# Sixteen squares of the feed-forward stage moved to POOL, one store for the last block, and a new written order

## The chip, the cores and the metric

The kernel runs on one core of a Trainium2 chip. It uses five engines that run side by side and meet through semaphores: PE (matmuls), DVE (the vector engine), ACT (the scalar engine), POOL (GpSimd) and SP, which here only issues DMAs. The metric is the device time of one execution in microseconds. The kernel before took 110.79 us (median of three runs, 110.61 to 112.53).

## What is computed

Two stages, the first feeding the second. The attention stage maps each query and key vector to a feature vector of 64 products and works with those linearly; the second stage is a feed-forward layer whose activation is the square of the positive part.

```python
def phi(x):                                   # 32 numbers -> 8 x 8 products
    a = np.einsum('rd,bhsd->bhsr', S1, x)
    b = np.einsum('rd,bhsd->bhsr', S2, x)
    return np.einsum('bhsi,bhsj->bhsij', a, b).reshape(*x.shape[:-1], r * r)
q_p, k_p = (phi(q), phi(k))                   # 4 batches, 4 heads, 1088 tokens, 64 features
kv = np.einsum('bhsf,bhsd->bhfd', k_p, v)
z = np.sum(k_p, axis=2)
num = np.einsum('bhsf,bhfd->bhsd', q_p, kv)
den = np.einsum('bhsf,bhf->bhs', q_p, z)[..., None] + 1e-06
x = num / den                                 # then laid out as 4352 tokens x 128
h = x @ w_in                                  # 128 -> 2048
r = np.maximum(h, 0.0)
g = r * r
out = g @ w_out                               # 2048 -> 128, float32
```

## The kernel before

**Attention.** The four batches are worked one after the other, overlapping. For batch b, `ldk`, `ldq` and `ldv` load keys, queries and values through SP's queue; `tk` and `tq` (L532 to L546, L697) transpose on DVE; `ksk` projects keys on PE; `kr` (L572) transposes the projections out of PSUM on DVE; `kp` (L580, L621) forms the 64 products on DVE, for one part of batch 0 on POOL; `vp` (L516, L519) copies the values beside a column of ones on POOL; `kv` (L643) accumulates on PE. Batches 0 and 1 form the query features from matmuls (`qr`, `qa` on ACT, `qp` at L752 on DVE). Batches 2 and 3 ("fold") go through memory: `ab` holds both projections, `zm`, `zt`, `zk`, `zb`, `dt`, `dr`, `dx` (POOL, L880) and `da` (L886) work the denominator in, `wr` stores to scratch memory, `rdA` (SP) and `rdB` (POOL) read it back repeated, and `qp2`, `qp3` (L927) multiply on DVE. `num` multiplies with `kv` on PE, `mx` and `tx` divide and transpose for batches 0 and 1, and `xe` puts the result as bf16 into `xT`, the input of the second stage. Small constants are made at the start: `zc` (L341 to L346) is eight scalings and two memsets on POOL.

**Feed-forward.** The 4352 tokens are cut into ten blocks, 256 tokens, seven times 512 and twice 256 (`SIZES`). Block n has up to nine steps m. A step is four operations, named in the order as `m1.n.m`, `r.n.m`, `g.n.m` and `m2.n.m`: `m1` (L1056) multiplies with two (for short blocks four) columns of tiles of `w_in` into a 128x1024 PSUM tile `h`; `r` (L1066 on ACT, L1068 on DVE) takes the positive part to bf16; `g` squares it (L1074 on ACT, L1076 on DVE); `m2` (L1090) multiplies with `w_out` and accumulates in PSUM, in the order of m. There are four buffers each for `r` and `g`, three for `h` and one accumulator for all blocks but the last. After the last step, `oe` (L1116) transposes the block out of PSUM to one of three output buffers `osb` on DVE, and `st` (L1126) stores it, four stores for each batch that the block touches. Block 9 is the exception: its `m2` (L1085) writes tokens in rows, and it is copied and stored in two halves (L1103, L1108).

**Order.** The order is written out. `PLAN` (L40 to L90) is one list of items `name:engine:buffers`; `Graph.run` (L124) emits each operation on the engine and into the buffers given there. Every engine, and every DMA queue, works through its own items in the order of the list, and waits where an input or a buffer is not there yet. The pairs of numbers at each `add(...)` are costs that only the program that found the order uses; they emit nothing. `HEAT` (L19) is a list of matmuls on zeros, by columns, that fill PE's time before the feed-forward stage.

Of the kernel before, what the change touches and what calls it, by code (L numbers as in the profile page):

```python
# [18 lines left out]
HEAT = [512] * 9 + [256] * 15  # L19
# [33 lines left out]
m1.1.3:PE:h1 g.1.0:ACT:g0 kp1.4:DVE qp1.1.0:DVE oe0:DVE:osb0 g.1.1:DVE:g1 ldq2.0:SP qp1.1.1:DVE vp1.1:POOL kv1.1:PE kve1.0:DVE r.1.3:ACT:r2 tk2.1:DVE
m1.1.5:PE:h2 r.1.5:ACT:r3 m2.1.0:PE:o0 ldv2.1:SP ldv2.0:SP tk2.0:DVE kve1.1:ACT m1.1.2:PE:h0 m1.1.4:PE:h1 kve1.2:ACT m2.1.1:PE g.1.3:DVE:g2
r.1.2:ACT:r1 m1.1.7:PE:h2 r.1.7:ACT:r0 r.1.4:ACT:r2 g.1.2:ACT:g3 tq2.0:DVE num1.0:PE:a0 st0.0.0:SP mx1.0:DVE:den0 ksk2:PE:h0 qr2:PE:h2 ab2:ACT
tx1.0:PE:a0 ldv2.2:SP m1.1.6:PE:h1 r.1.6:ACT:r1 xe1.0:ACT kr2:DVE m2.1.2:PE qr1.2:PE:h0:h2 qa1.2.0:ACT:A2 qa1.2.1:ACT:A1 ldv2.4:SP g.1.5:DVE:g0
ldv2.3:SP vp2.0:POOL ldk3.0:SP g.1.4:DVE:g1 vp2.1:POOL m2.1.3:PE kp2.0:DVE wr2.1.3:SP m1.2.4:PE:h1 r.2.4:ACT:r3 wr2.1.2:SP kp2.4:DVE m2.1.4:PE
tk3.1:DVE qp1.2.0:DVE kv2.0:PE:a0 qp1.2.1:DVE kv2.1:PE g.2.4:ACT:g3 kve2:ACT m1.2.0:PE:h1 r.2.0:ACT:r2 wr2.1.0:SP wr2.1.1:SP m1.2.2:PE:h0 m2.1.5:PE
tk3.0:DVE m1.2.1:PE:h2 zm2:DVE g.1.7:DVE:g2 ldq3.0:SP r.2.2:ACT:r3 g.1.6:DVE:g1 zt2:PE:a0 zk2:DVE tq3.0:DVE m1.2.6:PE:h1 m2.1.6:PE ldv3.4:SP zb2:PE:a0
r.2.6:ACT:r0 ldv3.2:SP dt2:DVE m2.1.7:PE oe1:DVE:osb1 ldv3.1:SP g.2.0:ACT:g0 m1.2.3:PE:h0 r.2.1:ACT:r1 num1.1:PE:h1.1 dr2:DVE ldv3.0:SP mx1.1:DVE:den1  # L60
num1.2:PE:a0 st0.0.3:SP r.2.3:ACT:r2 g.2.1:ACT:g1 qr3:PE:h2 ab3:ACT rdB2.544:POOL ksk3:PE:h0 st0.0.2:SP rdB2.0:POOL ldv3.3:SP g.2.2:ACT:g2
st1.256.3:SP dx2:POOL da2:DVE wr2.0.2:SP wr2.0.3:SP kr3:DVE m2.2.0:PE:o0 g.2.3:ACT:g0 mx1.2:DVE:den2 tx1.1:PE:h1.1 xe1.1:ACT m2.2.1:PE st1.256.1:SP
m1.2.7:PE:h2 r.2.7:ACT:r1 kp3.0:DVE m2.2.2:PE kp3.4:DVE m1.2.5:PE:h0 r.2.5:ACT:r3 g.2.5:DVE:g1 m2.2.3:PE m1.3.2:PE:h1 r.3.2:ACT:r2 g.2.6:DVE:g2
wr2.0.0:SP vp3.0:POOL kv3.0:PE:a0 m2.2.4:PE m1.3.1:PE:h2 g.2.7:DVE:g0 vp3.1:POOL r.3.1:ACT:r3 g.3.1:DVE:g3 m1.3.0:PE:h0 r.3.0:ACT:r0 m2.2.5:PE
wr2.0.1:SP tx1.2:PE:h1.1 m2.2.6:PE g.3.2:DVE:g1 m1.3.3:PE:h2 st0.0.1:SP m2.2.7:PE oe2:DVE:osb2 g.3.0:DVE:g2 m1.3.6:PE:h0 r.3.3:ACT:r1 kv3.1:PE zm3:DVE
g.3.3:DVE:g0 m1.3.5:PE:h2 zt3:PE:h1.0 r.3.6:ACT:r3 m1.3.4:PE:h0 m2.3.0:PE:o0 st1.256.0:SP kve3:ACT rdA2.0:SP zk3:DVE qp2.0:DVE st1.256.2:SP zb3:PE:a0
wr3.1.3:SP r.3.5:ACT:r2 m2.3.1:PE dt3:DVE dr3:DVE dx3:POOL r.3.4:ACT:r0 wr3.1.1:SP g.3.4:ACT:g2 num2.0:PE:h2 st2.768.2:SP m2.3.2:PE m1.3.7:PE:h0
xe2.0:ACT wr3.1.0:SP wr3.1.2:SP m2.3.3:PE r.3.7:ACT:r1 xe1.2:DVE m1.4.0:PE:h1 r.4.0:ACT:r0 m2.3.4:PE g.3.5:DVE:g3 m1.4.1:PE:h2 m2.3.5:PE da3:DVE
st2.1088.2:SP g.3.6:DVE:g1 m1.4.2:PE:h0 m2.3.6:PE rdA2.544:SP r.4.1:ACT:r2 r.4.2:ACT:r3 g.3.7:DVE:g0 qp2.1:DVE m1.4.5:PE:h1 st2.768.1:SP m2.3.7:PE
r.4.5:ACT:r1 g.4.0:DVE:g2 m1.4.4:PE:h2 num2.1:PE:h0 m1.4.3:PE:h1 r.4.4:ACT:r0 oe3:DVE:osb0 st2.1088.0:SP xe2.1:ACT wr3.0.3:SP m2.4.0:PE:o0  # L70
m1.4.6:PE:h2 g.4.1:DVE:g3 m2.4.1:PE g.4.2:DVE:g1 g.4.5:DVE:g0 r.4.3:ACT:r2 g.4.4:DVE:g2 wr3.0.2:SP m1.5.0:PE:h0 wr3.0.0:SP g.4.3:DVE:g3 m2.4.2:PE
r.4.6:ACT:r3 g.4.6:DVE:g1 m1.5.5:PE:h1 m2.4.3:PE m1.4.7:PE:h2 r.5.0:ACT:r1 m2.4.4:PE r.4.7:ACT:r0 wr3.0.1:SP m1.5.1:PE:h0 r.5.5:DVE:r2 m2.4.5:PE
m1.5.2:PE:h1 g.5.0:DVE:g3 rdB3.0:POOL g.4.7:DVE:g2 r.5.1:ACT:r3 r.5.2:ACT:r1 rdA3.0:SP m2.4.6:PE m1.5.3:PE:h2 qp3.0:DVE m2.4.7:PE oe4:DVE:osb1
rdB3.544:POOL rdA3.544:SP m1.5.4:PE:h0 g.5.2:DVE:g0 r.5.3:ACT:r0 st4.2176.3:SP g.5.1:ACT:g1 num3.0:PE:h1 xe3.0:DVE r.5.4:ACT:r1 m2.5.0:PE:o0
g.5.3:DVE:g2 m1.5.6:PE:h2 g.5.5:DVE:g3 st4.1792.0:SP st4.1792.1:SP st2.768.0:SP m2.5.1:PE m1.6.0:PE:h1 st2.1088.1:SP st2.1088.3:SP r.5.6:ACT:r3
m2.5.2:PE g.5.4:DVE:g1 m1.5.7:PE:h0 g.5.6:DVE:g0 r.6.0:ACT:r0 qp3.1:DVE m2.5.3:PE m1.6.1:PE:h2 st3.1280.0:SP m2.5.4:PE g.6.0:DVE:g2 r.5.7:ACT:r2
# [74 lines left out]
def pe(t):  # L151
    return (t, t + 0.17)
# [3 lines left out]
def kernel(  # L156
# [1021 lines left out]
```

## Time and profile before

| | |
|---|---|
| runs | 110.79 us median (110.61 to 112.53) |
| profiled execution, own time | 110.52 us |
| its span, first to last instruction | 108.7 us |
| granted TensorE clock, mean | 0.997 |
| POOL copies `vp` of 128x512 | 7, median 614 ns |
| DVE squares `g` | 56, mean 688 ns |
| ACT squares `g` of 128x1024 | 11, mean 1066 ns |
| ACT `r` of 128x1024 | 63, mean 1032 ns (13 in a row take 12.29 us) |

The span runs from the first to the last instruction on the chip; the execution's own time also holds what lies around it, 1.8 us here. Busy times add up the durations of instructions; an instruction starts some 0.08 us before the one ahead of it on its engine has ended, so durations of single instructions are a little longer than their spacing. An instruction that has started and then waits for something inside its engine counts as busy.

### The profile page before, as it was taken

The page shows a single profiled execution, that of the slowest core. Times are in us where ns is not written, and L with a number is a line of the kernel's source. Part 1 is how long each engine was busy: PE and PEld are TensorE (multiplying, and loading weights), DVE is VectorE, ACT ScalarE, POOL GpSimd, SP SyncE. Part 2 cuts the span into 40 slices and gives each one's busy share as a digit, 9 for nine tenths or more (in the row PEclk, how much of TensorE's full clock was granted, in tenths as well). Part 3 has the DMA queues.
Part 4 walks back from the last instruction along what each step waited for, and adds up shares of the span by engine and source line. Part 5 has one row for each costly group of instructions (what it writes and reads, how often), then busy time and mean ns, then how long its engine had stood idle before and what let it go on. Part 6 is the DMA issues. An engine that isn't in the chain of part 4 may idle for free.

```text
span 108.7 us, 3616 instructions
## 1 busy us (share of the span) xinstructions
PE 98.1 (90%) x1438; PEld 56.9 (52%) x1438; DVE 94.1 (87%) x175; ACT 87.6 (81%) x123; POOL 31.4 (29%) x72
## 2 busy tenths in 40 slices
PE   5968999999999997899899999998999999997920
PEld 2355786766655373565546334443444445575920
DVE  5388499999999999699999989997999999996730
ACT  2226463979999999879889998989899999999900
POOL 4914993560005378015800099000000000000000
PEclk9999999999999999999999999999999999999998
DMA  2896999994164189993472358878244000336641
GB/s 53 225 214 195 359 178 252 283 247 140 18 148 178 52 240 205 205 215 80 68 222 64 103 141 229 233 206 201 48 77 80 1 0 0 54 55 104 114 76 39
DMA packets 27025, 15.23 MB, mean 140 GB/s; under 512 B 19712, under 2 KB 24448, under 8 KB 27008
## 3 DMA queue, kind: packets, MB, share of 16 engines
q1 hardware_dynamic: 23976, 11.58, 43.1%
q0 software_dynamic: 2272, 3.28, 15.0%
q8 instruction: 11, 0.18, 0.8%
q10 hardware_dynamic: 760, 0.14, 0.6%
q14 instruction: 6, 0.05, 0.1%
HBM read 13.25 MB, written 2.79 MB: 147 GB/s over the span
## 4 chain that ended last, share of the span: by engine, by line
DVE 43%; PE 27%; issue 8%; SPq 8%; DMA 6%; POOL 1%; ACT 1%; DVEq 1%; POOLq 0%
DVE g L1076 15%; PE o L1090 9%; PE h L1056 6%; DVE kp L580 6%; SPq L1126 4%; DMA vin<-in_v_dram 4%; DVE osb L1116 3%; DVE kT L532 3%; DVE qp L927 2%; PE h L643 2%; DVE qp L752 2%; DVE kt L572 2%; PE h L716 2%; DVE qT L697 2%; DVE xs L1013 2%
## 5 line engine op out<-in xcount | busy, mean ns | idle before, releaser
L1066 ACT ACTIVATE r<-h 128x1024 bf16<-128x1024 f32 x63 | 60.9, 1032 | 4.1 <-PE h L1056 2.2
L1090 PE MATMUL o<-g,w_out 128*128 128x512 bf16 (+1 forms) x144 | 38.3, 356 | 2.2 <-issue 1.1
L1056 PE MATMUL h<-xT,w_in 128*128 128x512 bf16 (+1 forms) x156 | 39.0, 350 | 0.4 <-ACT xT L1031 0.2
L1076 DVE TENSOR_TENSOR g<-r 128x1024 bf16<-128x1024 bf16 x56 | 36.2, 688 | 0.5 <-ACT r L1066 0.2
L1056 PEld LDWEIGHTS <-w_in 128*128 128x128 bf16 x160 | 17.3, 115 | 14.4 <-issue 2.1
L1090 PEld LDWEIGHTS <-w_out 128*128 128x128 bf16 x144 | 13.2, 97 | 14.9 <-issue 5.7
L1074 ACT ACTIVATE g<-r 128x1024 bf16<-128x1024 bf16 (+1 forms) x13 | 12.8, 998 | 0.2
L516 POOL COPY vp<-vin 128x512 f32<-128x512 f32 x7 | 5.2, 769 | 19.2 <-PE h L564 10.4
L914 POOL DMA_DIRECT2D Bq<-scr x16 | 9.0, 595 | 2.2 <-DMA scr<-ab 2.2
L580 DVE TENSOR_TENSOR kp<-kt 128x1024 f32<-128x1024 f32 (+1 forms) x6 | 8.5, 1435 | 0.0
L752 DVE TENSOR_TENSOR qp<-h,A 128x256 f32<-128x256 f32 (+3 forms) x16 | 6.3, 428 | 2.1 <-ACT A L738 2.0
L738 ACT COPY A<-h 128x256 f32<-128x256 f32 (+3 forms) x16 | 5.4, 406 | 2.8 <-PE h L716 2.1
L353 PE MATMUL o<-zero 128*128 128x256 bf16 (+1 forms) x24 | 6.1, 398 | 1.2 <-DVE mk L276 1.2
L1116 DVE STREAM_TRANSPOSE osb<-o 128x512 f32<-128x512 f32 (+1 forms) x9 | 5.8, 648 | 1.2 <-DMA out_dram<-osb 0.8
L716 PE MATMUL h<-qT,SR 32*64 32x192 f32 (+2 forms) x176 | 6.4, 340 | 0.0
L643 PEld LDWEIGHTS a<-vp,kp 128*32 128x32 f32 x432 | 4.5, 109 | 2.6 <-issue 2.5
L927 DVE TENSOR_TENSOR qp<-qp,Bq 128x1088 f32<-128x1088 f32 x4 | 5.2, 1288 | 0.6 <-DMA qp<-scr 0.6
L643 PE MATMUL a<-vp,kp 128*32 128x33 f32 x432 | 5.2, 198 | 0.5 <-POOL vp L519 0.3
L697 DVE STREAM_TRANSPOSE qT<-qin 128x1088 f32<-128x1088 f32 (+5 forms) x7 | 5.5, 803 | 0.0
L880 POOL COPY dnT<-dnr 128x288 f32<-128x288 f32 x2 | 1.3, 674 | 13.0 <-DVE dnr L875 8.7
L519 POOL COPY vp<-vtl 32x128 f32<-32x128 f32 x6 | 5.0, 836 | 0.2
L1068 DVE TENSOR_SCALAR r<-h 128x1024 bf16<-128x1024 f32 x4 | 4.8, 1215 | 0.0
(114 smaller groups left out, 105.5 us busy)
## 6 DMA issues: line engine op xcount, KB each, us to landing
Bq<-scr POOLq DMA_DIRECT2D x16, 136.0 KB, 5.1
qp<-scr SPq DMA_DIRECT2D x8, 272.0 KB, 4.7
vin<-in_v_dram SPq DMA_DIRECT2D x16, 128.0 KB, 4.5
kin<-in_k_dram SPq DMA_DIRECT2D x3, 544.0 KB, 4.0
qin<-in_q_dram SPq DMA_DIRECT2D x3, 544.0 KB, 5.0
out_dram<-osb SPq DMA_DIRECT2D x17, 64.0 KB, 1.9
scr<-ab SPq DMA_DIRECT2D x16, 34.0 KB, 2.2
kin<-in_k_dram SPq DMA_DIRECT2D x2, 256.0 KB, 3.2
```

The costliest lines, as they stand in the source:

```text
L580: (nc.vector if e == "DVE" else nc.gpsimd).tensor_tensor(out=kp[i][:, k0:k1].rearrange("p j h (x y) -> p (j h) x y", y=R), in0=v[:, :, 1, ...
L643: nc.tensor.matmul(t[p : p + KW, 33 * (h // 2) : 33 * (h // 2) + 33], kp[i][:, j, h, KW * f : KW * f + KW], vp[i][:, h, j, :], start=(j == ...
L697: nc.vector.transpose(qT[i][:, 32 * c0 : 32 * c1], qin[i][:, 32 * c0 : 32 * c1])
L716: nc.tensor.matmul(at(hb[h // 2])[lo : lo + 64, 512 * s + 256 * x : 512 * s + 256 * x + ns[s]], SR[32 * h : 32 * h + 32, x].rearrange("p x ...
L752: nc.vector.tensor_tensor(out=o, in0=pv, in1=av, op=ALU.mult)
L914: (nc.sync if e == "SP" else nc.gpsimd).dma_start(out=Bq[i][64 * m : 64 * m + 64, pr, s0:s1], in_=scr[i][1][8 * (2 * pr + m) : 8 * (2 * pr ...
L1056: nc.tensor.matmul(at(hb)[:, c : c + N], w_in[:, 512 * (ct // E) : 512 * (ct // E) + 512].rearrange("p (c e) -> p e c", e=E)[:, ct % E], x ...
L1066: nc.scalar.activation(o, s, ACTF.Relu)
L1074: nc.scalar.activation(at(gb)[:, 0 : W * N], r, ACTF.Square)
L1076: nc.vector.tensor_tensor(out=at(gb)[:, 0 : W * N], in0=r, in1=r, op=ALU.mult)
L1090: nc.tensor.matmul(at(ob)[:, 0:N], w_out[:, ct, :], at(gb)[:, N * w : N * w + N], start=(ct == 0), stop=(ct == CT - 1))
L1116: nc.vector.transpose(at(sbuf)[:, 0:N], at(ob)[:, 0:N])
```

## The change

- Sixteen of the 69 squares go to POOL: `g.1.0`, `1.3`, `1.4`, `1.6`, `2.4`, `2.6`, `3.2`, `3.5`, `3.6`, `4.5`, `5.0`, `5.1`, `6.0`, `6.3`, `6.6` and `7.5`. DVE keeps 42 of its 56, ACT 11 of its 13. On POOL they are the same multiplication of `r` with itself.
- Block 9 is copied out of PSUM at once (`oe9`) and stored with one DMA (`st9.0`). For this the columns of `xT` for the last 256 tokens stand in another order, so that a row of the store is 1024 bytes instead of 512.
- All stores are issued by SP; three were on ACT.
- There are five output buffers `osb` instead of three.
- The matmuls on zeros are 18 of up to 512 columns (8640 columns in all) instead of 24 (8448 columns).
- The whole order is new. Among other things `zc` moves from the start to behind `g.1.0` on POOL, `vp0.0` goes to ACT and `vp0.1` to POOL, `kp0.7` and `SKw` come ahead of the loads of the weights, `num0.0` comes ahead of `qr0.2`, six `r` instead of five are on DVE (3.1, 3.5, 5.1, 6.0, 6.6 and 8.0), and `tq1.0` comes ahead of `qp0.1`.
- A new mode `foldp` and its tables are added, but no batch uses it; some of the planner's costs are changed.

```diff
-HEAT = [512] * 9 + [256] * 15
+HEAT = [512] * 9 + [448] * 1 + [512] * 4 + [192] * 1 + [512] * 2 + [320] * 1
...
-        "r": one("r", NR), "g": one("g", NR), "osb": one("osb", 3), "den": one("den", 3), "A": one("A", 3),
+        "r": one("r", NR), "g": one("g", NR), "osb": one("osb", 5), "den": one("den", 3), "A": one("A", 3),
...
-                    fn(xT[:, t1 + 288 : t1 + 544].rearrange("p (x t c) -> p x c t", x=2, c=4),
-                       at(nb)[:, 528:784].rearrange("p (x c t) -> p x c t", x=2, c=4))
+                    fn(xT[:, t1 + 288 : t1 + 544].rearrange("p (x t c) -> p c x t", x=2, c=4),
+                       at(nb)[:, 528:784].rearrange("p (c x t) -> p c x t", x=2, c=4))
...
-                    nc.vector.tensor_tensor(out=at(gb)[:, 0 : W * N], in0=r, in1=r, op=ALU.mult)
+                    (nc.vector if e == "DVE" else nc.gpsimd).tensor_tensor(out=at(gb)[:, 0 : W * N], in0=r, in1=r, op=ALU.mult)
...
-            for x in range(N // 128):
-                c0 = (n0 - S * b) // 32 + 4 * x
...
-                    fn(at(sbuf)[:, 0:128], at(ob)[:, 128 * x : 128 * x + 128])
...
-                        out=out[S * b : S * b + S, :].rearrange("(t c) d -> t c d", c=C)[:, c0 : c0 + 4, :],
-                        in_=at(sbuf)[:, 0:128])
+            c0, w = (n0 - S * b) // 32, N // 32
+            sbuf = Buf("osb")
...
+                fn(at(sbuf)[:, 0:N], at(ob)[:, 0:N])
...
+                    out=out[S * b : S * b + S, :].rearrange("(t c) d -> t c d", c=C)[:, c0 : c0 + w, :].rearrange(
+                        "t (c x) d -> t c (x d)", x=2),
+                    in_=at(sbuf)[:, 0:N])
+            add(f"st{n}.0", {"SP": (0.65, 3.0)}, f_st, [o_oe], uses=[sbuf], dma=0.4)
...
-                if n >= len(SIZES) - 2:
-                    al["ACT"] = (0.55, 3.0)
```

The new order of POOL from block 1 on, and of DVE from `oe0` to `oe7`, read out of the new list:

```
POOL  z1 vp1.0 vp1.1 g.1.0 zc g.1.4 g.1.3 g.1.6 vp2.0 vp2.1 g.2.4 vp3.0 rdB2.0 dx2 rdB2.544 g.2.6
      vp3.1 g.3.2 g.3.5 g.3.6 dx3 rdB3.0 g.4.5 g.5.0 g.5.1 rdB3.544 g.6.0 g.6.3 g.6.6 g.7.5
DVE   oe0 qp1.1.1 qp1.1.0 tk2.0 tk2.1 g.1.2 mx1.0 tq2.0 g.1.5 kr2 tk3.1 kp2.0 tk3.0 kp2.4 g.2.2
      qp1.2.1 zm2 qp1.2.0 zk2 tq3.0 dt2 dr2 oe1 da2 mx1.1 kr3 kp3.0 mx1.2 r.3.1 g.3.1 kp3.4 r.3.5
      oe2 zm3 kve3 zk3 qp2.0 dt3 dr3 g.3.4 da3 g.3.7 qp2.1 g.4.0 oe3 g.4.1 xe2.1 g.4.2 g.4.3 g.4.6
      g.4.4 r.5.1 g.4.7 qp3.0 oe4 xe3.0 g.5.3 g.5.5 g.5.4 r.6.0 g.5.6 g.5.7 qp3.1 oe5 g.6.1 g.6.2
      r.6.6 g.6.4 g.6.5 g.7.1 g.6.7 g.7.0 oe6 g.7.2 g.7.3 g.7.4 r.8.0 g.7.6 g.8.0 g.7.7 g.8.2 oe7
```

173 lines of the change are left out of this document (102 added, 71 removed).

## The prediction

> **What bounds the kernel now.** I read the busy shares first, then the slices, the chain, and windows over the two stretches that the change works in.
>
> ```profile
> PE 98.1 (90%) x1438; PEld 56.9 (52%) x1438; DVE 94.1 (87%) x175; ACT 87.6 (81%) x123; POOL 31.4 (29%) x72
> ...
> DVE 43%; PE 27%; issue 8%; SPq 8%; DMA 6%; POOL 1%; ACT 1%; DVEq 1%; POOLq 0%
> ```
>
> DVE carries 43% of the chain and is 87% busy; POOL is 29% busy and, by the slices, empty after 69 us. Moving squares there looks free. The windows cut at the block copies: `oe0` ends near 28.5, `oe3` at 68.2, `oe7` at 100.1.
>
> ```profile
> 28.50:68.20 39.70, 37.88 (x719) 20.41 (x716) 37.69 (x71) 37.13 (x52) 16.59 (x26) 1.00 0.63 150
> 68.20:100.10 31.90, 30.70 (x179) 15.69 (x178) 30.18 (x46) 30.83 (x36) 0.00 (x0) 1.00 0.40 86
> ```
>
> The columns are length, then PE, PEld, DVE, ACT and POOL busy. In both stretches PE, DVE and ACT are all within 3 us of full, so a microsecond added to any of the three lengthens the stretch by nearly that much.
>
> **Is POOL independent of DVE?** Three moments in the timelines say no (start, duration, instruction):
>
> ```profile
> 34.54 1.03 DVE L1076 TENSOR_TENSOR g<-r 128x1024 bf16<-128x1024 bf16 x1
> 34.42 0.61 POOL L516 COPY vp<-vin 128x512 f32<-128x512 f32 x1
> ...
> 62.66 0.68 DVE L1076 TENSOR_TENSOR g<-r 128x1024 bf16<-128x1024 bf16 x1
> 62.69 0.92 POOL L880 COPY dnT<-dnr 128x288 f32<-128x288 f32 x1 [8.67 <-DVE dnr L875]
> ...
> 47.51 0.42 POOL L880 COPY dnT<-dnr 128x288 f32<-128x288 f32 x1 [4.37 <-DVE den L1010]
> 47.69 0.56 DVE L1013 TENSOR_TENSOR xs<-h,rec 128x384 bf16<-128x384 f32 x1
> ```
>
> The POOL copy ends at 34.42 + 0.61 = 35.03; the square begun at 34.54 ends at 35.57, 0.54 us later, which is what a square (0.65 alone) needs after its start-up: it stood still until POOL was done. At 62.69 it is the other way: POOL's copy takes 0.92 instead of 0.42 because the square holds it. At 47.69 nothing is held: that DVE operation takes one input from PSUM. So a DVE instruction with **both inputs in SBUF** and a POOL instruction that reads SBUF exclude each other for their whole length. In that class on DVE are the squares `g` (0.60 us from start to start in a run), `kp1` to `kp3` (1.07 to 1.33), `qp2`, `qp3` (1.21) and the product of `da`. Outside it are `oe` (0.64), `r` (1.14), `xe` (0.63), transposes and whatever reads PSUM. POOL's DMA issues hold nobody: squares beside them at 64.5 to 67.6 take the usual 0.68.
>
> The Trainium skill, "SBUF — State Buffer", section "Who interferes with whom", states this as an exclusive lock between a VectorE instruction with two SBUF inputs and any GpSimd instruction that reads SBUF; the rows agree for copies, and no row here has a POOL TENSOR_TENSOR beside such a DVE instruction. By it the forecast's mechanism holds; if it held for copies only, the first rival would be the result.
>
> **Price of one square on POOL.** The trace has none. The nearest row is a POOL product of two SBUF inputs, running beside DVE work of the free class:
>
> ```profile
> 10.41 1.07 POOL L621 TENSOR_TENSOR kp<-kb,ka 128x512 f32<-128x512 f32 x1
> ```
>
> Twice the elements give 2.14 us, the upper end. If bf16 halves it, as on DVE (0.60 for 1024 bf16 against 1.21 for 1088 f32), it is 1.07, the lower end. I take 2.1: same operation, same two reads.
>
> The Trainium skill, "GPSIMD Engine Reference", section 3.1, gives 4497 ns for 2048 f32 elements, so an estimate of 2.25 us here, and its section 4.1 advises against such work on this engine; by that figure the sum would be about 1.5 us longer.
>
> **The sum, against the profiled execution's 110.52 us** (0.27 under the median 110.79 of the runs shown).
>
> *From `oe3` to `oe7`, 31.9 us now.* DVE's own work in the new order: 25 squares x 0.60, 4 `r` x 1.14, `qp3.0` and `qp3.1` 2.4, 4 `oe` x 0.64, 2 `xe` x 0.63 = 25.8 us (now 30.2). ACT: 28 `r` x 0.95 (13 in 12.29 us), one square 1.06, `xe3.1` 1.3 = 29.0; PE 32 pairs of second and first matmuls x 0.87 and two `num` x 0.6 = 29.0. Without the lock the stretch would take some 29.5. With it, I walk down the two orders by hand, t counted from the end of `oe3`; DVE and POOL take turns where both wait:
> - square 4.5 holds the lock 0.6 to 2.7; `g.4.2`, due at 1.2 after `xe2.1`, stands 1.5
> - 5.0 holds 5.1 to 7.2; `r.5.1` runs, `g.4.7` stands 1.0
> - 5.1 holds 7.8 to 9.9; `qp3.0` stands 2.1
> - 6.0 holds 15.9 to 18.0; `g.5.7` stands 2.1
> - 6.3 holds 19.8 to 21.9; `oe5` runs, `g.6.1` stands 1.5
> - 6.6 holds 24.9 to 27.0; `g.6.5` stands 2.1
> - 7.5 holds 30.6 to 32.7; `g.7.3` stands 2.1
>
> Together 12.4 us, so 25.8 + 12.4 = 38.2: **+6.3**. Even with the best alignment the locked classes alone need 15 + 2.4 + 7 x 2.1 = 32.1 us: no gain is possible here at that price.
>
> *From `oe0` to `oe3`, 39.7 us now.* DVE loses nine squares (5.4), `kve1.0` and `xe1.2` (0.5), gains `r.3.1`, `r.3.5` (2.3) and `kve3` (about 0.5): relief 3.2. Stalls: 1.0 none (beside `qp1.1`, `tk2`); 1.4 holds `g.1.5` 1.9; 1.3 holds `kp2.0` 0.7; 1.6 holds `kp2.4` 1.5; `vp2.0`, now right behind, 0.3 more than today; `zc`, eight operations of 0.30 to 0.37 moved here from the start, 0.2; 2.4 none (beside `dt2`, `dr2`); 2.6 holds `g.3.1` 1.0; 3.2, 3.5 and 3.6 in a row hold `qp2.0` 2.1 and `g.3.4` 0.9. Together 8.6, less 3.2 = +5.4; half of DVE's 2.0 us of pauses there absorbs 1.0: **+4.4**.
>
> *Start.* `vp0.0` changes places with `vp0.1`; `kp0.7` comes ahead of the weights; `num0.0` no longer stands behind `qr0.2` (1.07 us of PE); `tq1.0` (0.54) can fill DVE's pause at 11.4 to 13.0. Between -1.1 and +0.7 (a late gate for the weights); I take **-0.5**. Zero matmuls: 24 become 18, 8448 columns become 8640, in PE time that waits for loads anyway: 0. `zc`'s old place (2.2 to 4.8) was idle. Should a weight come late instead, the row "waits for w_in" shows 0.3 today.
>
> *`osb` 3 to 5.* It removes this wait, which sits inside the 31.9 and which the walk does not have:
>
> ```profile
> 99.41 0.72 DVE L1116 STREAM_TRANSPOSE osb<-o 128x512 f32<-128x512 f32 x1 [0.83 <-DMA out_dram<-osb]
> ```
>
> Next late after it is the square itself, so it brings nothing of its own beyond the walk.
>
> *End.* Two copies (0.28 each) become one of twice the width, between 0.28 and 0.45. But the four stores of block 8 (two of them on ACT now) all stand ahead of `st9.0` on SP: `oe8` ends 103.69, four issues of about 0.45 end near 105.5, `st9.0` takes 0.64 to 106.15. Today ACT's `st9.1` is issued until 106.16. **0**, between -0.9 (SP free at once) and +1 (older stores still queued on SP). The changed x columns of the last 256 tokens keep the size of their copy (0.76): 0. The new planner costs and the `foldp` branch emit nothing here.
>
> 110.5 - 0.5 + 4.4 + 6.3 = 120.7, say **121 us**.
>
> **Rivals.**
> 1. *No lock for a POOL TENSOR_TENSOR, or squares that always fall beside free work.* Then the relief is kept: 2.4 in the late stretch (31.9 to 29.5, ACT and PE the next bounds), 2.5 of the 3.2 in the early one (ACT sheds only two `r` there), 0.5 at the start: 105.1. For it: the order places 1.0 and 2.4 beside long runs of free DVE work. Against: the held copies, and that seven squares x 2.1 find only 8.4 us of free DVE work in the late stretch. It decides from a mean stall under 0.3 us per square. Chance 0.16.
> 2. *Squares near the lower end, 1.07 us.* The stalls of the walk shrink to 0.4 + 0 + 4 x 1.0 + 0.4 = 4.8: the late stretch takes 30.6, the early one about as long as now, 109 to 111 in all. For it: DVE's bf16 rate. Against: no POOL row shows a type that goes faster. Chance 0.16.
> 3. *The order degenerates*: a late square on POOL makes PE, whose second matmuls run in block order, wait beside DVE, and stalls average a full 2.1: 16 x 2.1 = 33.6 less 7.6 of relief: up to 136. Waits overlap, so I give all beyond 127 a chance of 0.07, inside the slower case.
>
> **How the numbers follow.** Forecast and third rival 0.68 together, rivals 1 and 2 0.16 each. Two per cent is about what a measurement of this kernel can tell (its runs lie between 110.61 and 112.53). Faster 0.16, within 2% 0.16, slower 0.68. The range from 107.5 to 127 leaves out most of rival 1 and the far tail; it takes in both ends of the square's price. The forecast's own range is 115 to 127.
>
> **What would show it.** Right: POOL squares of 2.1 us or more in the groups, DVE squares (now 688 ns on average) near 1 us, with some near 2.7; DVE's busy time above 100 us although it does less, since a held instruction counts as busy; the stretch from `oe3` to `oe7` near 38 us. Wrong: DVE squares still near 0.7 us and DVE under 90 us (rival 1), or POOL squares near 1.1 (rival 2). The prediction fails if long free runs on DVE line up with the POOL squares more often than my walk has it.

## The result and the profile after

The changed kernel takes **120.96 us** (median of 4 runs, 118.84 to 122.96); the kernel before, in the same job, 111.66 (110.61 to 113.07). The ratio is 1.079, 95% interval 1.054 to 1.104: slower, by about 9 us. The forecast was 121. The profiled execution is the longest of the four, 122.96 us, with a span of 121.2 us against 108.7 before. Executions over 1.5% longer than the fastest of the same kernel, here two of the four, stand outside the ratios.

The page of the changed kernel, in the lines that answer to those of before (busy shares, the clock row of the slices, the chain, and the two groups of squares; L1112 is the line of `g` that was L1076):

```profile
PE 99.6 (82%) x1419; PEld 56.4 (47%) x1432; DVE 103.2 (85%) x163; ACT 85.3 (70%) x117; POOL 66.3 (55%) x90
...
PEclk9999999999999999999999999998599999999999
...
DVE 30%; issue 16%; PE 15%; POOL 11%; ACT 11%; SPq 6%; DMA 6%; ACTq 1%; DVEq 0%; POOLq 0%
...
L1112 POOL TENSOR_TENSOR g<-r 128x1024 bf16<-128x1024 bf16 x16 | 33.1, 2076 | 22.7 <-PE o L1126 9.7
...
L1112 DVE TENSOR_TENSOR g<-r 128x1024 bf16<-128x1024 bf16 (+1 forms) x42 | 37.3, 916 | 2.3 <-ACT r L1102 1.2
```

The DVE squares of the kernel before:

```profile
L1076 DVE TENSOR_TENSOR g<-r 128x1024 bf16<-128x1024 bf16 x56 | 36.2, 688 | 0.5 <-ACT r L1066 0.2
```

DVE has 14 squares fewer and is busy for 9.1 us **more** (94.1 before): 42 squares now take 916 ns on average, 56 took 688. That is the mark of instructions that have started and are held. POOL's 16 squares take 2.08 us each. PEclk shows one dip to half speed, which is followed up below.

Windows cut as before, at the ends of `oe0`, `oe3` and `oe7`; I call the four pieces front, early, late and tail (columns: length, then busy time of PE, PEld, DVE, ACT, POOL with counts, clock, DMA share, GB/s):

```profile
0.00:32.64 32.64, 25.43 (x562) 17.06 (x566) 24.28 (x55) 16.52 (x31) 15.43 (x41) 1.00 0.71 175
32.64:72.49 39.85, 36.67 (x640) 19.86 (x640) 38.12 (x65) 35.43 (x49) 34.14 (x39) 1.00 0.52 136
72.49:112.34 39.85, 32.93 (x176) 16.00 (x178) 36.53 (x38) 29.39 (x34) 16.78 (x11) 0.96 0.41 87
```

| span of the profile, us | front | early | late | tail | sum |
|---|---|---|---|---|---|
| before | 28.49 | 39.75 | 31.89 | 8.62 | 108.75 |
| after | 32.64 | 39.85 | 39.85 | 8.82 | 121.16 |
| difference | +4.15 | +0.10 | +7.96 | +0.20 | +12.41 |

So two thirds of the loss lie in the late stretch and one third in the front; the early stretch, in which eight of the sixteen squares run, pays nothing on balance (square 1.0 runs ahead of `oe0`, in the front).

One pair of the late stretch, DVE first and then POOL, each from its own timeline (start, duration):

```profile
89.46 2.98 DVE L1112 TENSOR_TENSOR g<-r 128x1024 bf16<-128x1024 bf16 x2
92.37 1.28 DVE L963 TENSOR_TENSOR qp<-qp,Bq 128x1088 f32<-128x1088 f32 x1
...
89.70 2.20 POOL L1112 TENSOR_TENSOR g<-r 128x1024 bf16<-128x1024 bf16 x1 [5.52 <-PE o L1126]
```

POOL starts at 89.70 while DVE's first square runs and gets its turn when that is done; it ends at 91.90. DVE's second square ends at 89.46 + 2.98 = 92.44, which is 0.54 us after POOL: the same 0.54 that the square beside the POOL copy showed in the kernel before. I add up such excess as **held time**: the duration of a DVE instruction less what the same one takes where nothing holds it (square 0.68, `qp2` and `qp3` 1.285, `kp` 1.14 for 1024 elements and 1.41 for 1280). It is 1.6 us in the kernel before and 16.1 us after, 10.0 of it in the late stretch, 4.3 in the early one and 1.7 in the front.

### The profile page after: what moved, and what is told of

Its sections match the earlier page's. It is cut to its first block, busy times and chain, and to the rows that moved or that the text cites. A ratio compares the mean times of both kernels' runs of the same rounds, so it can differ in the third digit from the quotient of the medians.

```text
span 121.2 us, 3583 instructions
## 1 busy us (share of the span) xinstructions
PE 99.6 (82%) x1419; PEld 56.4 (47%) x1432; DVE 103.2 (85%) x163; ACT 85.3 (70%) x117; POOL 66.3 (55%) x90
## 3 DMA queue, kind: packets, MB, share of 16 engines
q1 hardware_dynamic: 24520, 11.71, 38.2%
## 4 chain that ended last, share of the span: by engine, by line
DVE 30%; issue 16%; PE 15%; POOL 11%; ACT 11%; SPq 6%; DMA 6%; ACTq 1%; DVEq 0%; POOLq 0%
DVE g L1112 9%; ACT r L1102 8%; DVE qp L963 6%; POOL g L1112 4%; DMA vin<-in_v_dram 4%; PE h L1092 4%; DVE r L1104 3%; SPq L1161 3%; POOL ZE L343 3%; PE h L727 3%; DMA out_dram<-osb 2%; DVE osb L1151 2%; PE h L654 2%; POOL vp L527 2%; PE o L1126 2%
## 5 line engine op out<-in xcount | busy, mean ns | idle before, releaser
L1102 ACT ACTIVATE r<-h 128x1024 bf16<-128x1024 f32 (+1 forms) x62 | 59.7, 1019 | 12.8 <-PE h L1092 4.7
L1112 POOL TENSOR_TENSOR g<-r 128x1024 bf16<-128x1024 bf16 x16 | 33.1, 2076 | 22.7 <-PE o L1126 9.7
L1126 PE MATMUL o<-g,w_out 128*128 128x512 bf16 (+1 forms) x140 | 38.0, 362 | 4.7 <-DVE g L1112 4.6
L1112 DVE TENSOR_TENSOR g<-r 128x1024 bf16<-128x1024 bf16 (+1 forms) x42 | 37.3, 916 | 2.3 <-ACT r L1102 1.2
L1126 PEld LDWEIGHTS <-w_out 128*128 128x128 bf16 x144 | 13.8, 99 | 18.1 <-issue 8.3
L1110 ACT ACTIVATE g<-r 128x1024 bf16<-128x1024 bf16 x11 | 11.6, 1062 | 0.1
L591 DVE TENSOR_TENSOR kp<-kt 128x1024 f32<-128x1024 f32 (+1 forms) x6 | 10.5, 1749 | 0.0
L1104 DVE TENSOR_SCALAR r<-h 128x1024 bf16<-128x1024 f32 x6 | 7.3, 1216 | 1.1 <-PE h L1092 1.1
L963 DVE TENSOR_TENSOR qp<-qp,Bq 128x1088 f32<-128x1088 f32 x4 | 7.9, 1976 | 0.0
L363 PE MATMUL o<-zero 128*128 128x512 bf16 (+3 forms) x16 | 5.8, 491 | 1.4 <-DVE zero L269 1.2
L530 POOL COPY vp<-vtl 32x128 f32<-32x128 f32 x8 | 5.5, 689 | 0.2
```

The costliest lines, as they stand in the source:

```text
L591: (nc.vector if e == "DVE" else nc.gpsimd).tensor_tensor(out=kp[i][:, k0:k1].rearrange("p j h (x y) -> p (j h) x y", y=R), in0=v[:, :, 1, ...
L963: nc.vector.tensor_tensor(out=qp[i][:, :, t0 : t0 + n], in0=qp[i][:, :, t0 : t0 + n], in1=Bq[i][:, :, t0 : t0 + n], op=ALU.mult)
L1102: nc.scalar.activation(o, s, ACTF.Relu)
L1104: nc.vector.tensor_scalar_max(o, s, 0.0)
L1110: nc.scalar.activation(at(gb)[:, 0 : W * N], r, ACTF.Square)
L1112: (nc.vector if e == "DVE" else nc.gpsimd).tensor_tensor(out=at(gb)[:, 0 : W * N], in0=r, in1=r, op=ALU.mult)
```

## The experiments

### The changed kernel once more

The same file, to see what of the above repeats.

> The changed kernel as it is, for a second profile. If the lock between POOL squares and DVE instructions with both inputs in SBUF sets the time, the DVE excess over unheld durations is again 14 to 18 us (16.2 by the first profile after) and the time 118 to 121. The first profile also has two pieces that the lock doesn't explain: 2.0 us in which PE issued nothing near 22 us, and half TensorE clock for 3 us near 85 us. If they belong to the change they come again; if not, this run is about 2 to 3 us under the first profile's 122.96.

Measured: 120.24 us (119.26 to 121.32; before in the same job 110.83, 109.03 to 112.2). Pieces 30.44, 40.17, 39.86 and 8.80 us; held time 16.5. The late stretch and its held instructions repeat to 0.01 us. The front does not: it is 2.2 us shorter. 0.9 of this lies ahead of the first `r` of the feed-forward stage; behind it, what is missing is a pause of PE that the first profile of the change has:

```profile
PE h L727 <- issue: 2.0, 1, 2.0
```

(The waits of PE, changed kernel, first profile: line, cause, total, times, longest.) PE stands 2.0 us before a matmul of `qr1.0` near 21.8 us and waits for nothing that the profile shows. The variants of the new order below have the same pause with 0.6 to 2.5 us, those of the order before with 0.1 to 0.9; the kernel before has none and this repeat 0.1. It always stands ahead of the same matmul of its order, and in all twelve of these profiles, with a pause or without, that matmul starts 1.4 to 1.7 us after a transfer of 16 KB in the queue that the profile calls "q8 instruction" has landed (22.21 and then 23.81 in the first profile, 19.44 and then 21.01 in the repeat). So PE most likely waits there for its own next instructions; no run changed that transfer, and why it comes earlier or later stays open.

### POOL writes but reads almost nothing

Sixteen squares become a copy of two columns and two fills on POOL, as long as a square together; the squares themselves are left out, so the output is not the reference's.

```diff
-  (nc.vector if e == "DVE" else nc.gpsimd).tensor_tensor(out=at(gb)[:, 0 : W * N], in0=r, in1=r, op=ALU.mult)
+  if e == "DVE":
+      nc.vector.tensor_tensor(out=at(gb)[:, 0 : W * N], in0=r, in1=r, op=ALU.mult)
+  else:
+      nc.gpsimd.tensor_copy(at(gb)[:, 0:2], r[:, 0:2])
+      for z in (1024, 1024):
+          nc.gpsimd.memset(at(gb)[:, 0:z], 0.0)
```

> The sixteen squares on POOL are replaced by a copy of two columns of r and two memsets of the g tile (the squares are left out, so blocks 1 to 7 lack those terms); POOL still waits for r and still takes an estimated 1.7 us for each, but it reads almost nothing. Lock theory: DVE squares fall from 916 ns back to about 690 ns, the 16.2 us of held time go, and the time falls to 104 to 109. Rival, lateness (PE waits because a square on POOL comes 1.9 us after r instead of 0.7): the time stays at 116 to 120. Rival, the new order is long by itself: 116 or more too.

Measured: 109.52 us (109.16 to 110.36; before 110.83). Its groups of squares and fills, and its late window (68.72 is the end of `oe3`):

```profile
L1117 POOL MEMSET g<- 128x1024 bf16 x32 | 30.4, 951 | 1.9
...
L1113 DVE TENSOR_TENSOR g<-r 128x1024 bf16<-128x1024 bf16 (+1 forms) x42 | 27.1, 669 | 2.5 <-PE o L1131 1.1 <-ACT r L1102 0.7
```

```profile
68.72:99.76 31.04, 30.00 (x176) 15.67 (x178) 27.05 (x38) 28.81 (x34) 17.95 (x26) 1.00 0.54 115
```

POOL is as busy in the late stretch as with squares (17.95 against 16.78 us), in the same places of the same order, yet DVE's squares are back at 669 ns, held time is 1.2 us and the stretch is 8.8 us shorter (7.1 us shorter than the 38.17 that the same squares give at full clock, in `early_dve` below). That takes the rest of the new order out of the list of causes for the late stretch: it is what POOL *reads* that costs. The Trainium skill, "SBUF — State Buffer", section "Who interferes with whom", says just this, that a DVE instruction with two SBUF inputs contends with a GpSimd instruction that reads SBUF and not with one that only writes it; 32 fills beside squares of 669 ns agree.

My figure for the time was too low (104 to 109). Even with nothing on POOL that holds DVE, the stretch takes 31.04 us, because PE is then busy for 30.00 of them and the relief of DVE (3 us) has nowhere to go. This run is the nearest thing to rival 1 of the prediction, and it lies 4 us above that rival's 105.1.

### All squares on DVE, in the new order

The sixteen items are changed from POOL to DVE in the list, nothing else; all of `g` is again on DVE and ACT.

```diff
-... g.4.5:POOL:g0 ... g.5.0:POOL:g3 ... g.5.1:POOL:g0
+... g.4.5:DVE:g0 ... g.5.0:DVE:g3 ... g.5.1:DVE:g0
...
```

> The new order with all sixteen squares back on DVE at the places they have in the list. Lock theory: minus 16.2 us of held time, plus 16 x 0.60 = 9.6 us of DVE work, so 119.5 - 6.6 = about 113 (110 to 114). Rival, the new order is long by itself: 117 or more. Lateness would give about what the lock gives; the run before this one tells those two apart.

The profiled execution ran with matmuls of twice the usual duration throughout (239.83 us; L1126 took 760 ns on average instead of 362), so its profile says nothing here. That trace records no granted clock, and its pairs of 512-column matmuls come some 1.2 us apart instead of 0.43, which is more than the half clock that the next expectation names; its cause stays open. The three others took 118.05, 115.65 and 115.33 us, above the expected 110 to 114. I ran the same file again:

> The same edit as the run named all_dve, for a profile that can be read: there PE ran at half clock through the whole profiled execution. The lock is gone there, and yet it takes 115 to 118 and not 111, so the new order costs about 5 us with its squares on DVE. Theory, head of line: the squares that were written for POOL stand in the list behind their r, and on DVE everything behind them waits for that r; then DVE's busy time is 96 to 99 and its pauses in blocks 1 to 7 grow from 4 us before to 8 or more. Rival, the rest of the order is longer whatever the squares do: excluded by the 109.5 of the run with writes only unless the POOL stage is empty here; then pauses would lie on PE with DVE idle beside it.

Measured: 114.58 us (113.43 to 115.11; before 110.72, 109.07 to 111.98), ratio 1.042, interval 1.028 to 1.055. Its early and late windows:

```profile
30.77:71.96 41.19, 37.44 (x657) 19.84 (x645) 39.68 (x75) 35.35 (x50) 15.04 (x31) 1.00 0.51 136
71.96:104.42 32.46, 30.60 (x179) 15.69 (x178) 30.66 (x45) 29.35 (x34) 0.92 (x2) 1.00 0.48 102
```

Two things follow. The squares on POOL are worth 121.2 - 113.2 = 8.0 us of the 12.4 us that the profiles differ by, or 119.3 - 113.2 = 6.1 by the repeat's profile; the late stretch alone loses 7.4 in both, 5.7 at full clock (the 38.17 of `early_dve` below). And the new order is 4.5 us longer than the old one even without a square on POOL: +2.3 us in the front, +1.4 early, +0.6 late, +0.2 in the tail. In the front, 1.4 lie before the first `r` of the feed-forward stage, which starts at 19.68 here and anywhere from 18.0 to 19.7 in the profiles with this front, and 0.9 are PE's pause; both differ between two executions of one kernel, so no item of the order is shown to cost them. DVE's pauses are only 1.5 and 1.8 us in these two windows, so squares that stand in front of others and wait for their `r` are not the reason; DVE is just full (39.68 of 41.19), as it was.

### Each square in two halves

```diff
-  (nc.vector if e == "DVE" else nc.gpsimd).tensor_tensor(out=at(gb)[:, 0 : W * N], in0=r, in1=r, op=ALU.mult)
+  en, k = (nc.vector, 1) if e == "DVE" else (nc.gpsimd, 2)
+  for x in range(k):
+      y = slice(W * N * x // k, W * N * (x + 1) // k)
+      en.tensor_tensor(out=at(gb)[:, y], in0=at(rb)[:, y], in1=at(rb)[:, y], op=ALU.mult)
```

> Each POOL square is cut into two instructions of 512 columns, about 1.0 us each. If the lock lasts for one whole instruction and the two engines take turns, no DVE square is held longer than about 1.0 us: the longest DVE square falls from 2.38 us to 1.7 or less, while the sum of held time stays within 13 to 18 us and the time within 117 to 121, since DVE gets in between but then meets the second half. If the engines shared the port by the element instead, nothing but some 1.5 us of POOL start-up would change and the longest DVE square stays near 2.4 us.

Measured: 118.58 us (118.43 to 119.44). The late stretch is 36.57 us instead of 39.85, the held time there 9.0 instead of 10.0. Three POOL halves beside two DVE operations (DVE, then POOL):

```profile
86.97 1.53 DVE L1115 TENSOR_TENSOR g<-r 128x1024 bf16<-128x1024 bf16 x1
88.42 2.12 DVE L963 TENSOR_TENSOR qp<-qp,Bq 128x1088 f32<-128x1088 f32 x1
...
87.91 4.98 POOL L1115 TENSOR_TENSOR g<-r 128x512 bf16<-128x512 bf16 x3
```

The square is 0.85 us longer than its 0.68 and `qp3.1` 0.84 longer than its 1.285, in place of one of 1.7: the two engines take turns, one instruction each, and a half costs half. Most of the held time comes in such steps of 0.84. The sum is nearly the same (15.1 us in all): what counts is how long POOL reads altogether while DVE has a locked instruction next. If the engines shared the port by the element, the square beside a half would not have gone back from 2.38 to 1.53. I had expected no square over 1.7 us; one of 2.56, held by 1.88, stands at 34.47, beside three halves in a row on POOL.

### Only the early squares, only the late squares

Seven items of blocks 4 to 7 back on DVE:

```diff
-... g.6.0:POOL:g1 ... g.6.3:POOL:g0 ... g.6.6:POOL:g2 ... g.7.5:POOL:g2
+... g.6.0:DVE:g1 ... g.6.3:DVE:g0 ... g.6.6:DVE:g2 ... g.7.5:DVE:g2
```

> Only the seven squares of blocks 4 to 7 go back to DVE. Lock theory: about 10 of the 16.2 us of held time lie there, against 7 x 0.6 = 4.2 us of DVE work; the stretch from oe3 to oe7 shrinks from 39.9 us to 32 to 34, the time from 119.5 to 112 to 114. Rival (lateness of the early squares, or the front, carries the loss): 117 or more.

Measured: 115.12 us (113.71 to 115.53), ratio 1.044, interval 1.028 to 1.060: above the expected 112 to 114, with the stretch inside its 32 to 34. And the nine items of blocks 1 to 3 back on DVE:

```diff
-... g.1.0:POOL:g1 ... g.1.4:POOL:g3 ... g.2.4:POOL:g2 ... g.3.2:POOL:g0
+... g.1.0:DVE:g1 ... g.1.4:DVE:g3 ... g.2.4:DVE:g2 ... g.3.2:DVE:g0
```

> Only the nine squares of blocks 1 to 3 go back to DVE. Lock theory: 5.7 us of held time (1.65 of it on kp1.4) against 9 x 0.6 = 5.4 us of DVE work, so next to no change: 118 to 121, with the stretch from oe3 to oe7 still near 39.9 us.

Measured: 122.13 us, above the expected 118 to 121: 119.29 in the profiled execution, at a granted clock of 1.000, and 121.37 to 123.39 in the other three, at 0.962 to 0.976. The late windows of the two, first without and then with the late squares on POOL:

```profile
71.64:104.67 33.03, 30.60 (x179) 15.67 (x178) 30.66 (x45) 29.35 (x34) 1.86 (x4) 1.00 0.50 103
```

```profile
70.36:108.53 38.17, 31.58 (x179) 15.67 (x178) 36.44 (x39) 29.28 (x34) 16.77 (x11) 1.00 0.41 87
```

In the same order of everything else, the seven late squares cost 38.17 - 33.03 = 5.1 us at full clock, the nine early ones nothing that the total shows: the profile of `late_dve`, which has them on POOL, spans 113.5 us, that with all squares on DVE 113.2. In the early stretch they even gain, 39.62 us with them on POOL (`late_dve`) against 40.80 on DVE (`early_dve`):

```profile
32.02:71.64 39.62, 37.27 (x647) 19.93 (x640) 38.08 (x65) 35.42 (x49) 34.43 (x40) 1.00 0.52 139
```

```profile
29.56:70.36 40.80, 37.35 (x647) 19.77 (x640) 39.28 (x74) 35.26 (x50) 13.67 (x29) 1.00 0.51 137
```

DVE's own work there is 5.0 us less (nine squares of 0.60) and the held time 3.8 us more; the front loses about as much again, as shown further below.

### The same squares on POOL in the order of the kernel before

The kernel before, its list unchanged but for the engine of the sixteen items.

```diff
-... g.1.3:DVE:g2 ... g.1.4:DVE:g1 vp2.1:POOL ... g.2.4:ACT:g3 ... g.5.0:DVE:g3 rdB3.0:POOL
+... g.1.3:POOL:g2 ... g.1.4:POOL:g1 vp2.1:POOL ... g.2.4:POOL:g3 ... g.5.0:POOL:g3 rdB3.0:POOL
```

> The kernel before, in its own order, with the same sixteen squares on POOL and nothing else changed. Lock theory: the held time is a property of the two engines and not of the new order, so it is again 14 to 20 us, DVE squares again average 0.85 us or more, and the time is 116 to 122. Rival, only the new order puts them badly: under 113.

Measured: 129.09 us (128.89 to 131.89), ratio 1.175, interval 1.158 to 1.193: worse than the change, and worse than expected by 7 us. Held time is 15.1 us, near the change's 16.1. What comes on top shows in POOL's own queue (waits of POOL, then of PE):

```profile
POOL g L1076 <- ACT r L1066: 15.9, 5, 6.4
...
PE h L944 <- issue: 6.0, 1, 6.0
PE a L643 <- POOL vp L516: 5.5, 2, 3.5
```

A square that waits for its `r` stands in front of the copies `vp` and of the DMAs `rdB`, and PE waits for both: the 6.0 us end when `qp3.0` is done, which started 4.67 us late for want of `rdB`. After such pauses PE is granted half its clock, for 10.2 us in all before the end of the late stretch. So part of what the new order does, it does for POOL's queue: it puts `vp` and `rdB` ahead of squares that are not ready.

### Only the seven late squares, in the order of the kernel before

```diff
-... g.4.5:DVE:g0 ... g.5.0:DVE:g3 rdB3.0:POOL ... g.5.1:ACT:g1 ... g.6.0:DVE:g2 ... g.6.3:DVE:g0 ... g.6.6:ACT:g1 ... g.7.5:DVE:g3
+... g.4.5:POOL:g0 ... g.5.0:POOL:g3 rdB3.0:POOL ... g.5.1:POOL:g1 ... g.6.0:POOL:g2 ... g.6.3:POOL:g0 ... g.6.6:POOL:g1 ... g.7.5:POOL:g3
```

> The kernel before with its own order and all its other parts, and only seven of its squares moved to POOL: 4.5, 5.0, 5.1, 6.0, 6.3, 6.6 and 7.5, the same seven that the change moves in blocks 4 to 7 (5.1 and 6.6 from ACT, the other five from DVE). The lock theory: each of the seven holds one DVE square for up to 1.9 us, so DVE's held time grows by 8 to 12 us and its own work falls by 3.0: the stretch from oe3 to oe7, 31.9 before, becomes 37 to 41, and the two others stay within 0.8 us: 116 to 120 us in all. A rival, that the loss came of the order found anew and the squares on POOL alone are harmless: a stretch of 31 to 33 us, 110 to 112 in all.

Measured: 121.61 us (121.02 to 123.65), ratio 1.095, interval 1.088 to 1.103, with a late stretch of 42.04 us. Both theories miss: the time is over 120, the stretch longer than 41, and the held time in it only some 5 us. The stretch can't be set beside the others as it stands: this profile has a clock of 0.85 from 6.7 us on and 0.79 in the late stretch, and PE is busy for 26.82 of its last 26.98 us. But POOL's timeline shows a second cause:

```profile
70.32 1.89 POOL L1076 TENSOR_TENSOR g<-r 128x1024 bf16<-128x1024 bf16 x1 [4.20 <-ACT r L1066]
75.79 1.90 POOL L1076 TENSOR_TENSOR g<-r 128x1024 bf16<-128x1024 bf16 x1 [3.57 <-ACT r L1066]
77.62 4.48 POOL L914 DMA_DIRECT2D Bq<-scr  x8
```

In the kernel before these eight DMAs of `rdB3` were issued at 63.57; here they stand behind two squares that wait for their `r`, at 77.62. `qp3.0` started 4.75 us late for want of them, and PE stood 5.6 us until it was done. I repeated it with both `rdB3` ahead of the first of the squares:

```diff
-... g.4.2:DVE:g1 g.4.5:POOL:g0 ... g.5.0:POOL:g3 rdB3.0:POOL ... rdB3.544:POOL rdA3.544:SP
+... g.4.2:DVE:g1 rdB3.0:POOL rdB3.544:POOL g.4.5:POOL:g0 ... g.5.0:POOL:g3 ... rdA3.544:SP
```

> As before_late (the order of the kernel before, and only the seven squares 4.5, 5.0, 5.1, 6.0, 6.3, 6.6 and 7.5 on POOL), but both rdB3 are issued on POOL ahead of square 4.5, as they were issued ahead of all of block 4's squares before. In before_late a square that waited 3.57 us for its r stood in front of them; qp3.0 started 4.75 us late and PE stood 5.56 us for it, so that run mixed two causes. The lock theory now alone: DVE's own work between oe3 and oe7 falls from 30.2 by 3.0, held time grows by 7 to 11 us: a stretch of 35 to 39 us at full clock (31.9 before), 114 to 118.5 us in all, and no PE wait over 2.5 us. A rival, that the whole loss of before_late was the late read: a stretch of 31 to 33 us and 110 to 112 us in all.

Measured: 115.94 us (114.67 to 117.6; before 110.24, 109.69 to 111.39), ratio 1.051, interval 1.042 to 1.059. Its late window, and one pair (DVE, then POOL):

```profile
70.17:107.18 37.01, 32.88 (x179) 15.95 (x178) 34.63 (x41) 29.10 (x34) 14.63 (x7) 0.95 0.35 74
```

```profile
77.81 2.98 DVE L927 TENSOR_TENSOR qp<-qp,Bq 128x1088 f32<-128x1088 f32 x1
...
77.64 1.99 POOL L1076 TENSOR_TENSOR g<-r 128x1024 bf16<-128x1024 bf16 x1 [0.31 <-PE o L1090]
```

The stretch is 37.01 us (35 to 39 expected), +5.1 on before, of which a dip of PE's clock as in the change is about 1.7. In it five DVE instructions are held, by 1.64, 0.77, 1.69, 1.70 and 1.18, together 7.0 us, the lower end of what was expected; `qp3.0` above is one. So seven squares on POOL make the old order slower as well, by the same mechanism, and the slip in POOL's queue in the run before was worth about as much again (121.61 against 115.94 us, PE's lower clock after its pause included).

### The small parts alone

The kernel before with five `osb`, block 9 in one copy and one store, its columns, and all stores on SP; no square on POOL, the order as it was.

```diff
-"osb": one("osb", 3)
+"osb": one("osb", 5)
...
-oe9.0:DVE:osb1 st8.3840.2:ACT st8.3840.1:ACT oe9.1:DVE:osb2 ... st9.0:SP st9.1:ACT
+oe9:DVE:osb4 st8.3840.2:SP st8.3840.1:SP ... st9.0:SP
```

> The kernel before with its own order, and of the change only the small parts: five osb instead of three, block 9 copied at once and stored with one DMA, the x columns that go with it, and every store on SP. No square on POOL. By the prediction's terms: the wait of oe7 for a store (0.83 us) goes, and since the next thing late behind it is the square on DVE, nothing or up to 0.5 us comes of it; the end 0, between -0.9 and +1. So 110 to 111.5 us beside 110.8, no difference that can be measured, stretch from oe3 to oe7 31.4 to 32.0. A rival, that these parts carry a cost of their own that the order found anew only hid or paid for (SP's queue with all stores at the end): over 112, with a tail beyond oe7 above 9.3 us instead of 8.6.

Measured: 109.88 us (median of 12 runs, 109.5 to 112.9; before 110.92, 109.94 to 111.79), ratio 0.994, interval 0.990 to 0.998. That is just below the expected 110 to 111.5. `oe7` no longer waits (0.83 us before), and the late window is 1.07 us shorter:

```profile
98.42 0.72 DVE L1116 STREAM_TRANSPOSE osb<-o 128x512 f32<-128x512 f32 x1
```

```profile
68.31:99.13 30.82, 30.15 (x176) 15.66 (x178) 30.17 (x45) 30.02 (x35) 0.00 (x0) 1.00 0.39 88
99.13:108.10 8.97, 4.20 (x52) 3.47 (x49) 3.49 (x7) 3.81 (x6) 0.00 (x0) 1.00 0.42 80
```

The tail gives 0.3 of it back (8.92 us from `oe7` to the last instruction against 8.62; the second window reaches a little past it). This is the one version of the study that is faster than both kernels, by 0.6%, less than one run of each could tell.

## Why the prediction was right, point by point

**The lock: right, and shown.** POOL squares and fills of the same length, in the same order, differ by 8.8 us in the late stretch, 7.1 at full clock, and the held time goes from 16.1 us to 1.2 when POOL stops reading. The signs named beforehand came, two of them a little smaller: DVE busy above 100 us (103.2), DVE squares of about 1 us on average (0.916) with single ones up to 2.38 instead of 2.7, POOL squares of 2.08 on average instead of 2.1 or more, and the late stretch near 38 us (39.85; 38.17 at full clock in `early_dve`). It holds for POOL's TENSOR_TENSOR as for its copies.

**The price of a square: a little too high.** A square on POOL that nothing holds takes 1.89 us; I took 2.1, by doubling the row of 512 f32 elements, so the bounds 1.07 to 2.14 held and rival 2 fell. The Trainium skill's 4497 ns for 2048 f32 elements ("GPSIMD Engine Reference", section 3.1), from which I had estimated 2.25, is further off. In the walk 0.2 us too much seven times is 1.4 us.

**The late stretch: the right seven victims.** The walk by hand named which DVE instruction each POOL square would hold, and the profile has the same seven:

| square on POOL | held on DVE | forecast, us | measured, us |
|---|---|---|---|
| 4.5 | `g.4.2` | 1.5 | 1.36 |
| 5.0 | `g.4.7` | 1.0 | 0.78 |
| 5.1 | `qp3.0` | 2.1 | 1.69 |
| 6.0 | `g.5.7` | 2.1 | 1.70 |
| 6.3 | `g.6.1` | 1.5 | 1.06 |
| 6.6 | `g.6.5` | 2.1 | 1.70 |
| 7.5 | `g.7.3` | 2.1 | 1.70 |
| | sum | 12.4 | 9.99 |

The stretch grew by 7.96 and not by 6.3, though the stalls came to 2.4 us less. Three things that the step lacked make up the rest. DVE's own work is 36.53 - 9.99 = 26.5 instead of 25.8. DVE has pauses, which I had at nothing because I gave DVE the whole stretch: 1.7 us at full clock (38.17 - 36.44 in `early_dve`), of which 0.9 wait for an `r` on ACT and 0.6 for PE. Together with the smaller stalls that is 38.2, the forecast's own number, by errors that cancel. The last 1.7 us are PE's clock, below, and no term of the forecast had them.

**The early stretch: wrong, +0.1 instead of +4.4.** The step that failed is the sum of stalls, 8.6. Measured are 4.34: 1.63 on `g.1.2` by 1.4 (I had 1.9 on `g.1.5`), 0.42 each on `kp2.0` and `kp2.4` (0.7 and 1.5), 0.44 on `g.3.1` and 0.16 on `kp3.4` (1.0), 1.09 on `qp2.0` (2.1, and 0.9 on `g.3.4` that did not come), 0.09 each on `g.2.2` and `kp3.0`. I had also left out that the same stretch of the kernel before holds 1.35 us of such stalls already, beside the copies of `vp` and `dx`, most of which go away. DVE's own work fell by 2.6 us (36.4 to 33.8; the relief of 3.2 in the forecast is 3.1 by its own terms) and its pauses by 0.3, so +4.34 - 1.35 - 2.6 - 0.3 = +0.1. Here DVE has many operations that are not of the locked class, and the order laid POOL's squares beside them; so the first rival's second half, squares beside free work, is half true in this stretch.

**The start: wrong, +4.15 instead of -0.5.** One term is an error of the walk: I put square 1.0 beside `qp1.1` and `tk2`, behind `oe0`, at no cost. It runs ahead of `oe0`, at 28.44, and holds `kp1.4`:

```profile
28.58 3.09 DVE L591 TENSOR_TENSOR kp<-kt 128x1280 f32<-128x1280 f32 x1
...
28.44 1.89 POOL L1112 TENSOR_TENSOR g<-r 128x1024 bf16<-128x1024 bf16 x1 [2.52 <-issue]
30.32 2.11 POOL L343 TENSOR_SCALAR ZE<-RY,mk 128x32 f32<-128x32 f32 x1
```

(Changed kernel, DVE and then POOL; `kp1.4` takes 3.09 instead of 1.41, and the first scaling of `zc`, 0.36 elsewhere, is in turn held to 2.11.) The times of the first `r` of the feed-forward stage and of the end of `oe0`, with PE's pause taken out, sort the rest:

| profile | first `r`, us | from there to the end of `oe0`, us | of this PE's pause | the remainder |
|---|---|---|---|---|
| before | 18.32 | 10.17 | 0 | 10.17 |
| new order, square 1.0 not on POOL: `all_dve_2` | 19.68 | 11.09 | 0.93 | 10.16 |
| `early_dve` | 18.14 | 11.42 | 0.94 | 10.48 |
| `write_only` | 18.61 | 11.57 | 1.52 | 10.05 |
| with square 1.0 on POOL: `after_again` | 18.04 | 12.40 | 0.11 | 12.29 |
| `late_dve` | 19.74 | 12.28 | 0.60 | 11.68 |
| `halves` | 18.18 | 14.18 | 2.51 | 11.67 |
| changed kernel | 18.91 | 13.73 | 2.04 | 11.69 |

With the pause out, the rows fall into two groups by the lock alone, and the new order without it is where the kernel before is. (`after_again` lies 0.6 above its group; its held time in the front is 0.6 longer too.) So of the +4.15 us, 0.6 lie ahead of the first `r`, where the profiles with this front scatter by 1.7; 1.5 are the lock, near the 1.68 that `kp1.4` is held; 2.0 are PE's pause, which the forecast had no term for. The gain of 0.5 that I expected of the new order does not show.

**The rest.** The small parts, with the five `osb`, bring 1.07 us in the late stretch of the kernel before, where I had nothing "beyond the walk" for `osb`; that was a wrong step without weight here, since in the changed kernel DVE is late anyway. The end, forecast at 0, is +0.20, and +0.3 in the small parts alone. Rival 3 did not come: waits overlap, as said.

Taken together: 110.5 + 4.15 + 0.10 + 7.96 + 0.20 = 122.9, the profiled execution (122.96), and with the pieces of the repeat 110.5 + 1.95 + 0.42 + 7.96 + 0.18 = 121.0, its 121.04. The forecast of 121 had the mechanism right and, at full clock, the late stretch. That the total fits so well is luck: the early stretch was some 4 us too dear, the front 2.5 to 4.6 too cheap and the late stretch 1.7 too cheap, and these cancelled.

## What to carry to other kernels

A half-empty POOL is no free room for an elementwise operation when DVE runs operations with both inputs in SBUF: take the time that POOL would read as time that DVE stands, for each such operation that is next on DVE, and move work only if what lies beside it on DVE reads PSUM or has one SBUF input (with the exception named at the end). This kernel, whose DVE, PE and ACT are all within some 3 us of full, gained next to nothing from relieving one of them alone (109.52 us with fills on POOL, 110.83 before). And before anything is put on a queue that was nearly idle, look at what else is issued there: squares waiting in front of a DMA cost about as much as seven locks.

## What the runs showed of the hardware beyond that

**Half a clock after a pause of 1.9 us, by where the pause falls.** While `qp3.0` is held, PE has nothing to do. In the changed kernel and in `early_dve` the pause is the same to 0.01 us, and what comes after is not. First the changed kernel's PE, then that of `early_dve` (start and duration of two matmuls of 512 columns):

```profile
83.21 0.69 PE L980 MATMUL h<-qp,kvF 64*32 64x272 f32 x16 [1.93 <-ACT g L1110]
83.83 0.91 PE L1126 MATMUL o<-g,w_out 128*128 128x512 bf16 x2
84.54 1.06 PE L1092 MATMUL h<-xT,w_in 128*128 128x512 bf16 x2
85.39 1.06 PE L1126 MATMUL o<-g,w_out 128*128 128x512 bf16 x2
```

```profile
81.09 0.69 PE L980 MATMUL h<-qp,kvF 64*32 64x272 f32 x16 [1.92 <-ACT g L1110]
81.71 0.61 PE L1126 MATMUL o<-g,w_out 128*128 128x512 bf16 x2
82.16 0.59 PE L1092 MATMUL h<-xT,w_in 128*128 128x512 bf16 x2
82.59 0.60 PE L1126 MATMUL o<-g,w_out 128*128 128x512 bf16 x2
```

Pairs come every 0.86 us for some 3.5 us in the one and every 0.43 in the other. The late stretch is 39.85 and 38.17, so the dip costs 1.7 us; the repeat of the change has it too, `before_late_2` as well. The Trainium skill, "TensorE: Matmul & The Clock Gate", section "What's actually happening", gives an idle window of about 3.4 us for the drop to half rate. The traces agree on the length, but PE was busy for 1.43 of the 3.4 us before 83.2, so a window need not be idle throughout. They also show which window counts. In every trace with a recorded clock, the granted clock changes only after whole steps of 3.41 us from its first change (23 steps to 83.99 us in the changed kernel, then one step at 0.50, then ten at 1.00). PE's busy time in the steps that hold the pause:

| profile | step, us | PE busy in it, us | clock in the next step |
|---|---|---|---|
| changed kernel | 80.57 to 83.99 | 1.44 | 0.50 |
| its repeat | 79.15 to 82.56 | 1.49 | 0.50 |
| `before_late_2` | 78.56 to 81.97 | 1.49 | 0.50 |
| `early_dve` | 76.66 to 80.08 | 2.50 | 1.00 |
| `early_dve` | 80.08 to 83.49 | 2.40 | 1.00 |

In the first three the whole pause lies in one step; in `early_dve` it lies across the end of one (79.17 to 81.09), and the clock stays at 1.00. A held DVE instruction can thus cost more than its own length, through PE.

**What holds and what does not.** POOL's fills of 128x1024 bf16 take 0.951 us and hold no square. A scaling on DVE with one SBUF input of the denominators (`dr`, at 66.82 us in the changed kernel) took 0.405 us instead of 0.184 while POOL read, a case that the prediction's rule of two SBUF inputs does not cover.
